# A SwiGLU kernel on one core: products three and four of each Strassen unit in 64-row tiles, and a new order around them

## The chip, the cores and the metric

The kernel runs on one core of a Trainium2 chip. The metric is the device time of one execution in microseconds (us); the median of three runs is given. Engines: PE is TensorE (matmuls; PEld is its weight load), DVE is VectorE, ACT is ScalarE, POOL is GpSimd, SP is SyncE, which issues the DMAs.

## The reference

With x of 2048 x 512 and weights of 512 x 1376 and 1376 x 512, all bf16:

```
g = silu(x @ w_gate)
u = x @ w_up
return (g * u) @ w_down
```

## The kernel before, in words

**Tiling.** The 2048 rows of x are four chunks c of 512 (SC); x stands transposed in `xT_sb`, with the 512 features as four blocks of 128 partitions (KD = 4, KH = 2). The 1376 hidden columns are ten blocks ft of 128 (NFF) and a rest of 96. First phase: for every ft and c, gate and up are products of four matmuls of 128x128 weights on 128x512 data, silu and a multiplication give h (`h0_sb` for chunks 0 and 1, `h1_sb` for 2 and 3). Second phase (`down`): h times w_down, with four 32-row matmuls side by side in the array (`strips`, line 731), a part in whole matmuls (line 780), then copies and stores.

**Classic groups.** `classic(c, fts, own)` (line 452) computes gate and up of one block directly: two column tiles of 64 side by side (line 407) or, with banks of its own, whole matmuls (line 418); then silu on ACT and the multiplication on DVE. The rest of 96 columns goes through `plan_x`, `plan_y` and `y_out` (silu pieces into `sgx_sb` and `sgy_sb`, products into `htx_sb`, `hty_sb`, `hl_sb`).

**Strassen units.** A unit (pi, u) takes two blocks ft (f0, f1 = 2u, 2u+1) and two chunks (c0, c1 = 2pi, 2pi+1), for gate (m = 0) and up (m = 1). It needs seven products instead of eight. `w_sums` builds four sums of weight blocks (S1 to S4) and a copy of A22 in `ss_sb`, mostly on POOL; `x_sums` builds T1 to T4 and a copy of B22 in `tt_sb`. These are f32 values, and their products run in a one-pass f32 format: `four` (line 585, matmuls at line 590), for each m two matmuls (k = 0, 1) of 128x128 weights on 128x512 data. Products one and two use the bf16 operands: `two` (line 597, matmuls at line 602).

A unit has three pairs of PSUM banks, one bank for each m: X (banks 0, 1 or 2, 3 by turns), Y (4, 5) and W (6, 7). `p1` writes X; ACT copies X0 into Y0 and DVE X1 into Y1. `p6` adds S2 x T2 onto X, and ACT keeps X in `r_sb`. `p2` adds onto Y, and `direct` makes an h block of it: silu of the gate bank on ACT, times the up bank on DVE. `p5` writes S1 x T1 into W. `p7` adds S3 x T3 onto X, ACT keeps X again, and `sums` makes an h block: DVE adds the kept values and W into `ts_sb`, ACT takes silu, POOL multiplies. `p4` adds A22 x T4 onto X, then `direct`; `p3` adds S4 x B22 onto W, then `sums`.

**What sets the order.** The operations are recorded in a `Plan`. Those of TensorE and of SP keep the order in which the program states them; those of ACT, DVE and POOL are put in order by `schedule`, a list planner that takes the operation that can start first by stated costs (216 ns for a bf16 matmul, 231 for an f32 one, 485 on ACT, 610 on DVE), then by priority. `emit` adds the semaphore waits. A matmul group that needs a result of an earlier group of TensorE itself (`after`) also waits on TensorE's semaphore.

**The order on TensorE**, from line 835: classic groups, among them ft 0 to 3 of chunk 1 in 64-column tiles; `plan_x` and `plan_y`; p1 of unit 0; ft 4 of chunk 1 as whole matmuls in banks 6 and 7; then for each of seven units p6, p2, p5, p7, p1 of the next unit (in the last one ft 5 of chunk 1), p4, p3; then `down`.

Of the kernel before, what the change touches and what calls it, by code (L numbers as in the profile page):

```python
# [4 lines left out]
ACT = mybir.ActivationFunctionType  # L5
# [8 lines left out]
PE_STEP, PE_STEP4, PE_LAG = 216, 231, 205  # L14
A_BUSY, A_LAG = 485, 180
# [14 lines left out]
class Plan:  # L30
# [73 lines left out]
    def emit(self, engines, sems):  # L104
        for op in self.ops:
            for d in op.deps:
                if d.dma is None and not (d.eng == op.eng == "P" and d not in op.raw):
                    d.users += 1
        for e, ops in self.order.items():
            n = 0  # L110
            for op in ops:
                if op.dma is None and op.users:
                    n += 1
                    op.count = n
        known = {e: {} for e in self.order}
        ready = {}
        done = set()
        at = dict.fromkeys(self.order, 0)
        left = len(self.ops)
        plans = {e: [] for e in self.order}  # L120
        while left:
            moved = False
            for e, ops in self.order.items():
                while at[e] < len(ops) and all(d in done for d in ops[at[e]].deps):
                    op = ops[at[e]]
                    need = {}
                    for d in op.deps:
                        if d.dma is not None:
                            key, n = d.dma
                        elif d.eng == e == "P" and d not in op.raw:  # L130
                            continue
                        else:
                            key, n = d.eng, d.count
                        if known[e].get(key, 0) < n and need.get(key, (0, 0))[0] < n:
                            need[key] = (n, d)
                    implied = {}
                    for key, (n, d) in need.items():
                        for k, v in ready[d].items():
                            if k != key:
                                implied[k] = max(implied.get(k, 0), v)  # L140
                    waits = [(d.end, key, n) for key, (n, d) in need.items() if implied.get(key, 0) < n]
                    for key, (n, d) in need.items():
                        for k, v in ready[d].items():
                            known[e][k] = max(known[e].get(k, 0), v)
                    clock = dict(known[e])
                    if op.dma is not None:
                        clock[op.dma[0]] = max(clock.get(op.dma[0], 0), op.dma[1])
                    elif op.count:
                        clock[e] = max(clock.get(e, 0), op.count)
                    ready[op] = clock  # L150
                    plans[e].append((sorted(waits, key=lambda w: w[0]), op))
                    done.add(op)
                    at[e] += 1
                    left -= 1
                    moved = True
            assert moved
        for e, steps in plans.items():
            for waits, op in steps:
                for _, key, n in waits:
                    engines[e].wait_ge(sems[key], n)  # L160
                ins = op.emit(engines[e])
                if op.dma is not None:
                    ins.then_inc(sems[op.dma[0]], 16)
                elif op.count:
                    ins.then_inc(sems[e], 1)


def bass_standalone__swiglu_ffn__prompt_kernel(nc, x, w_gate, w_up, w_down, out):
# [4 lines left out]
    KH = KD // 2  # L173
# [11 lines left out]
    HC = P // 2  # L185
# [12 lines left out]
    with ExitStack() as es:  # L198
# [21 lines left out]
        sgy_sb = [sb(f"sgy_sb{i}", [P, SC], FP32) for i in range(2)]  # L220
        o_all = sb("o_sb", [P, NOS, D], BF16)
        ss_sb = sb("ss_sb", [P, NSLOT, 5, 2, KH, P], F32R)
        tt_sb = [tt0_sb, sb("tt1_sb", [P, 5, KH, SC], F32R)]
        psum = ps("psum", [P, NB, 512], FP32)
        turn = [0, 2, 1, 3, 4, 5, 6, 7]
        bank = lambda i: psum[:, i, :]
# [77 lines left out]
        for c in range(NSC):  # L304
            load(
                f"wdx{c}",
                lambda e, c=c: e.dma_start(wdt_sb[R * c:R * (c + 1), 1, :], w_down[F - R:F, :]),
                [f"wdx{c}"], 800, 300,
            )
        for i in range(2):  # L310
            load(
                f"wdy{i}",
                lambda e, i=i: e.dma_start(wdt_sb[2 * R * i:2 * R * (i + 1), 0, :], w_down[NFF * P:F - R, :]),
# [9 lines left out]
            b = A_BUSY if engs == "A" else D_BUSY  # L323
            return plan.add(engs, emit, reads, writes, busy or b, A_LAG if engs == "A" else D_LAG, prio, after=after)

        def silu_op(out, src, reads, writes, prio=5):
            return plan.add(
                "A", lambda e: e.activation(out, src, ACT.Silu), reads, writes, A_BUSY, A_LAG, prio  # L328
            )

        def tt_op(engs, out, a, b, alu, reads, writes, prio, busy, after=()):
# [9 lines left out]
        def pe(emit, reads, writes, n, step=PE_STEP, after=()):  # L341
            return plan.add("P", emit, reads, writes, int(n * step), PE_LAG, dma=None, after=after)
# [37 lines left out]
        for dk in range(KD):  # L380
            keys = [("b", 2 * dk), ("b", 2 * dk + 1)] if dk < KD - 1 else [("b", 6)]
            pe(transposes(dk), ["xn", "ident"], keys, 0.5)
            out, src = xT_sb[:, dk, 0:HT], tview_last()
            if dk < KD - 1:
                out, src = out.rearrange("p (i h t) -> p h i t", i=NXN, h=2), tview(dk)
            else:
                out = out.rearrange("p (i t) -> p i t", i=NXN)
# [64 lines left out]
        def classic(c, fts, own=None):  # L452
            gates = [next_bank() for ft in fts] if own is None else own[:1]
            ups = [next_bank() for ft in fts] if own is None else own[1:]
            for ft, b in zip(fts, gates):
                gu_group(0, ft, c, b, own is not None)
            for ft, b in zip(fts, ups):
                gu_group(1, ft, c, b, own is not None)
            for ft, bg, bu in zip(fts, gates, ups):
                classic_out(ft, c, bg, bu)  # L460
# [3 lines left out]
        def yblk(c):  # L464
            return (0, 64) if c % 2 == 0 else (64, 128)

        def plan_x(c, b):
            def emit(e):
                for dk in range(KD):
                    for m in (0, HC):  # L470
                        ins = e.matmul(
                            psum[m:m + HC, b, :], lhsT=w_sb[:, dk, 0, XC0 + m:XC0 + m + HC],
                            rhs=xT_sb[:, dk, c * SC:(c + 1) * SC],
                            start=(dk == 0), stop=(dk == KD - 1), tile_position=(0, m),
                        )
                return ins
            pe(emit, x_keys(c) + [f"wg{slab_of[NFF]}", "wut"], [("b", b)], KD)
            y0, y1 = yblk(c)
            sgx, kx = sgx_sb[c % 2], ("sgx", c % 2)
            silu_op(sgx[96:128, :], psum[64:96, b, :], [("b", b)], [kx], 4)  # L480
            silu_op(sgy_sb[c // 2][y0:y1, :], psum[0:64, b, :], [("b", b)], [("sgy", c)], 4)
            tt_op(
                "D", htx_sb[R * c:R * (c + 1), :], sgx[96:128, :], psum[96:128, b, :], ALU.mult,
                [kx, ("b", b)], [("htx", c)], 4, D_BUSY,
            )
            if c == LC:
                tt_op(
                    "D", hl_sb[2 * R:3 * R, :], sgx[96:128, SC - P:SC], psum[96:128, b, SC - P:SC], ALU.mult,
                    [kx, ("b", b)], [("hl", 2)], 4, 300,
                )  # L490
# [27 lines left out]
        W_SUM = {"S1": 0, "S2": 1, "S3": 2, "S4": 3, "A22": 4}  # L518
        X_SUM = {"T1": 0, "T2": 1, "T3": 2, "B22": 3, "T4": 4}
# [56 lines left out]
        class Unit:  # L576
# [61 lines left out]
                    self.two(m, KH, self.Y[m], False)  # L638
                self.direct(self.Y, self.f0, self.c0)

            def p4(self):
                for m in range(2):
                    self.four("P4", m, "A22", "T4", self.X[m], False)
                self.direct(self.X, self.f1, self.c0)

            def p3(self):
                for m in range(2):
                    self.four("P3", m, "S4", "B22", self.W[m], False)
                self.sums(2, self.f0, self.c1)

            def direct(self, b, ft, c):
                sg, ksg = ring("sg", sg_sb)
# [30 lines left out]
        for at in range(NST):  # L683
            j, c = divmod(at, NSC)
# [151 lines left out]
        early = [2 * u + i for u in range(NFF // 2) if u not in U_ORDER[0] for i in range(2)]  # L836
        sums = w_sums(0, 8, (), "A")
        for fts in [[2, 3]] + [[ft] for ft in early[4:]]:
            classic(0, fts)
        for ft in early[:-2]:  # L840
            classic(1, [ft])
        sums = x_sums(0, "D", 6, sums)
        for u in U_ORDER[0]:
# [16 lines left out]
        y_out(1, 3)  # L860
        unit = make(0)
        unit.p1()
        classic(1, early[-2:-1], [6, 7])
        for n in range(len(units)):
            unit.p6()
            free = 2 * (1 - n % 2)
            unit.p2()
            unit.p5()
            unit.p7()
            if n + 1 < len(units):  # L870
                after = make(n + 1)
                after.p1()
            else:
                classic(1, early[-1:], [free, free + 1])
            unit.p4()
            unit.p3()
            unit = after
        down()

# [32 lines left out]
```

## Time and profile before

| | |
|---|---|
| runs (us) | 117.9, 118.03, 118.01; median 118.01 |
| the profiled execution's own time | 118.01 us |
| its span, first to last instruction | 116.7 us |
| granted TensorE clock | 1.000 |
| TensorE busy | 113.5 us, 97% of the span |
| DVE, ACT, POOL busy | 55.5, 55.0, 54.1 us |

The profile is one execution. A group of the page has line, engine and operation, what is written and read, the tile of the array in use (rows*columns), the shape, the count, then busy time and the mean of one in ns, then the idle time ahead of it with what ended it. Matmuls overlap in the array, so the mean of one is longer than the distance from one to the next. In the timeline the first number is the start and the second the length, in us; neighbours of one group are merged with their count. The chain of work that ended last goes from the first instruction to the last, at each step over what was waited for.

### The profile page before, as it was taken

Reading aid. Unit: us, or ns where it says so; the run is one execution under the profiler, and the core shown is the slowest. Engines: PE = TensorE matmul, PEld = TensorE weight load, DVE = VectorE, ACT = ScalarE, POOL = GpSimd, SP = SyncE. Lnnn points to the kernel's source line nnn. Section 1 sums busy time; section 2 is a strip of 40 time slices with the busy share of each in tenths; the row PEclk is TensorE's granted clock in tenths of the full one; section 3 lists DMA queues with packets and bytes.
Section 4 is the critical chain, followed back from the end, with each engine's and each line's share of the span. In section 5 each row is a group of like instructions: output and inputs, shape, how many; then the busy total and the mean of one; then the engine's idle time right before and its main releaser. Section 6 shows DMA issues by size and latency. Waiting matters only on the chain.

```text
span 116.7 us, 2563 instructions
## 1 busy us (share of the span) xinstructions
PE 113.5 (97%) x1066; PEld 65.3 (56%) x1066; DVE 55.5 (48%) x87; ACT 55.0 (47%) x104; POOL 54.1 (46%) x71
## 2 busy tenths in 40 slices
PE   7999999999899999999999999999999999999993
PEld 2695555554467666666767676554444444444452
DVE  0104599655947766685949586570000030404331
ACT  5336275389848786767676777740000020303001
POOL 1484000699994999899999942343000000000000
DMA  3999999993000000000000000000000041050512
GB/s 84 231 275 267 232 277 191 224 357 107 0 0 0 0 3 8 0 0 0 3 0 0 0 0 0 0 6 0 6 0 6 0 140 45 7 178 32 192 45 90
DMA packets 17467, 8.77 MB, mean 75 GB/s; under 512 B 8624, under 2 KB 17328, under 8 KB 17456
## 3 DMA queue, kind: packets, MB, share of 16 engines
q1 hardware_dynamic: 17312, 8.51, 28.9%
q8 instruction: 8, 0.13, 0.5%
q10 hardware_dynamic: 144, 0.10, 0.3%
q14 instruction: 3, 0.02, 0.1%
HBM read 4.68 MB, written 2.10 MB: 58 GB/s over the span
## 4 chain that ended last, share of the span: by engine, by line
PE 86%; POOL 9%; DVE 2%; ACT 1%; issue 0%
PE psum L590 28%; PE psum L731 25%; PE psum L407 12%; PE psum L602 10%; POOL ss_sb L333 9%; PE psum L780 8%; PE psum L346 2%; PE psum L418 1%; DVE tt_sb L333 1%; DVE h_sb L333 1%; ACT sg_sb L328 1%; PE psum L369 0%; PE psum L376 0%; ACT ss_sb L524 0%; DVE o_sb L322 0%
## 5 line engine op out<-in xcount | busy, mean ns | idle before, releaser
L590 PE MATMUL psum<-tt_sb,ss_sb 128*128 128x512 f32 x140 | 37.9, 414 | 0.5 <-POOL ss_sb L333 0.5
L590 PEld LDWEIGHTS psum<-tt_sb,ss_sb 128*128 128x128 f32 x140 | 26.2, 188 | 7.9 <-POOL ss_sb L333 1.1
L731 PE MATMUL psum<-wd_sb,h_sb 32*128 32x512 bf16 x480 | 27.5, 374 | 0.0
L333 DVE TENSOR_TENSOR h_sb<-sg_sb,psum 128x512 bf16<-128x512 f32 x26 | 17.8, 686 | 15.6 <-ACT sg_sb L328 10.2
L333 POOL TENSOR_TENSOR h_sb<-sg_sb,ts_sb 128x512 bf16<-128x512 f32 x14 | 18.0, 1288 | 9.6 <-ACT sg_sb L328 9.5
L333 DVE TENSOR_TENSOR ts_sb<-r_sb,psum 128x512 f32<-128x512 f32 x28 | 17.9, 681 | 7.0 <-ACT r_sb L321 7.0
L321 ACT ACTIVATE r_sb<-psum 128x512 f32<-128x512 f32 x28 | 15.3, 595 | 12.3 <-PE psum L590 12.3
L322 DVE CAST o_sb<-psum 128x512 bf16<-128x512 f32 (+1 forms) x11 | 6.4, 604 | 30.2 <-PE psum L731 25.1
L333 POOL TENSOR_TENSOR ss_sb<-w_sb 128x256 fp32r<-128x256 bf16 x20 | 13.1, 673 | 15.4 <-DVE tt_sb L333 11.6
L731 PEld LDWEIGHTS psum<-wd_sb,h_sb 32*128 32x128 bf16 x480 | 12.0, 93 | 13.8 <-PE psum L731 0.9
L328 ACT ACTIVATE sg_sb<-psum 128x512 f32<-128x512 f32 x26 | 15.6, 599 | 8.6 <-PE psum L407 8.1
L321 ACT ACTIVATE o_sb<-psum 128x512 bf16<-128x512 f32 (+1 forms) x7 | 3.7, 580 | 32.5 <-PE psum L731 25.4
L407 PE MATMUL psum<-xT_sb,w_sb 128*64 128x512 bf16 (+1 forms) x192 | 18.4, 355 | 0.0
L407 PEld LDWEIGHTS psum<-xT_sb,w_sb 128*64 128x64 bf16 x192 | 11.3, 115 | 6.8 <-DVE xT_sb L322 0.2
L602 PE MATMUL psum<-xT_sb,w_sb 128*128 128x512 bf16 x56 | 14.5, 382 | 0.0
L328 ACT ACTIVATE sg_sb<-ts_sb 128x512 f32<-128x512 f32 x14 | 8.9, 635 | 1.4 <-DVE ts_sb L333 1.4
L780 PE MATMUL psum<-wd_sb,h_sb 128*128 128x512 bf16 (+2 forms) x60 | 8.9, 308 | 0.0
L602 PEld LDWEIGHTS psum<-xT_sb,w_sb 128*128 128x128 bf16 x56 | 4.4, 98 | 7.2 <-issue 3.9
L780 PEld LDWEIGHTS psum<-wd_sb,h_sb 128*128 128x128 bf16 x60 | 4.6, 98 | 4.6 <-issue 0.4
L333 POOL TENSOR_TENSOR ss_sb<-ss_sb,w_sb 128x256 fp32r<-128x256 f32 x10 | 6.6, 674 | 0.0
L333 POOL TENSOR_TENSOR ss_sb<-w_sb,ss_sb 128x256 fp32r<-128x256 bf16 x10 | 6.5, 677 | 0.0
L322 DVE COPY psum<-psum 128x512 f32<-128x512 f32 x7 | 4.8, 693 | 0.0
(44 smaller groups left out, 62.8 us busy)
## 6 DMA issues: line engine op xcount, KB each, us to landing
out_dram<-o_sb SPq DMA_DIRECT2D x15, 128.0 KB, 1.8
wd_sb<-in_w_down_dram SPq DMA_DIRECT2D x1, 1280.0 KB, 7.7
w_sb<-in_w_gate_dram SPq DMA_DIRECT2D x4, 256.0 KB, 4.2
w_sb<-in_w_up_dram SPq DMA_DIRECT2D x4, 256.0 KB, 4.5
w_sb<-in_w_gate_dram SPq DMA_DIRECT2D x1, 352.0 KB, 5.0
w_sb<-in_w_up_dram SPq DMA_DIRECT2D x1, 320.0 KB, 4.4
xn_sb<-in_x_dram SPq DMA_DIRECT2D x1, 256.0 KB, 2.8
wdt_sb<-in_w_down_dram SPq DMA_DIRECT2D x4, 32.0 KB, 5.9
```

Source lines behind the costliest of these rows:

```text
L321: return e.activation(out, src, ACT.Copy)
L322: return e.tensor_copy(out, src)
L328: "A", lambda e: e.activation(out, src, ACT.Silu), reads, writes, A_BUSY, A_LAG, prio
L333: engs, lambda e: e.tensor_tensor(out, a, b, alu), reads, writes, busy,
L346: e.matmul(bank(NB - 1), lhsT=ones_w, rhs=ones_m, start=True, stop=True)
L407: ins = e.matmul(psum[h:h + HC, b, n0:n1], lhsT=w_sb[:, dk, m, ft * P + h:ft * P + h + HC], rhs=xT_sb[:, dk, c * SC + n0:c * SC + n1], sta ...
L418: ins = e.matmul(bank(b), lhsT=w_sb[:, dk, m, ft * P:(ft + 1) * P], rhs=xT_sb[:, dk, c * SC:(c + 1) * SC], start=(dk == 0), stop=(dk == KD ...
L590: ins = e.matmul(bank(dst), lhsT=s[:, k, :], rhs=t[:, k, :], start=(start and k == 0), stop=(k == KH - 1), skip_group_check=True,)
L602: ins = e.matmul(bank(dst), lhsT=w_sb[:, k0 + k, m, f:f + P], rhs=xT_sb[:, k0 + k, c:c + SC], start=(start and k == 0), stop=(k == KH - 1) ...
L731: ins = e.matmul(psum[:, g["bank"], 0:c1 - c0], lhsT=h(r, g["t"]), rhs=w[R * r:R * (r + 1), c0:c1], start=(start and n == 0), stop=final, ...
L780: ins = e.matmul(psum[:, b, 0:c1 - c0], lhsT=hrows(fk, t, 0, P), rhs=wd_sb[:, fk, c0:c1], start=(start and n == 0), stop=(stop and n == NF ...
```

## The change

Products three and four of a unit become one step, `p34`. Each f32 matmul of 128 rows is split into two of 64 rows: rows 0 to 63 work on one of the two outputs (gate or up), rows 64 to 127 at the same time on the other, in another bank. In a second phase the halves are exchanged, so that each output gets its missing rows. The four halves run in the order W, X, W, X; each second half waits for the first half of its own banks (`mark`). All four outputs then end within the second phase.

Around it, p2 moves behind p5 and p7. The classic group of ft 3 in chunk 1 goes from the 64-column tiles to whole matmuls ahead of p6 of the first unit, and that of ft 4 from there to behind that p6, in banks 2 and 3. The planner's cost of the silu pieces in `plan_x` rises from 485 to 610.

```diff
-        def silu_op(out, src, reads, writes, prio=5):
+        def silu_op(out, src, reads, writes, prio=5, busy=A_BUSY):
...
-            silu_op(sgx[96:128, :], psum[64:96, b, :], [("b", b)], [kx], 4)
-            silu_op(sgy_sb[c // 2][y0:y1, :], psum[0:64, b, :], [("b", b)], [("sgy", c)], 4)
+            silu_op(sgx[96:128, :], psum[64:96, b, :], [("b", b)], [kx], 4, 610)
+            silu_op(sgy_sb[c // 2][y0:y1, :], psum[0:64, b, :], [("b", b)], [("sgy", c)], 4, 610)
...
-            def p4(self):
-                for m in range(2):
-                    self.four("P4", m, "A22", "T4", self.X[m], False)
+            def half(self, a, b, dst, phase, start, after):
+
+                def emit(e):
+                    for k in range(KH):
+                        for h, m in ((0, phase), (HC, 1 - phase)):
+                            ins = e.matmul(
+                                bank(dst[m]), lhsT=ss_sb[h:h + HC, self.slot, W_SUM[a], m, k, :],
+                                rhs=tt_sb[self.pi][h:h + HC, X_SUM[b], k, :],
+                                start=(start and phase == 0 and k == 0), stop=(phase == 1 and k == KH - 1),
+                                tile_position=(h, 0), skip_group_check=True,
+                            )
+                    return ins
+                keys = [("ss", self.slot, a, m) for m in range(2)]
+                keys += [("tt", self.pi, X_SUM[b], k) for k in range(KH)]
+                return pe(emit, keys, [("b", d) for d in dst], KH, PE_STEP4, after)
+
+            def p34(self):
+                mark = [(), ()]
+                for phase in range(2):
+                    for i, (a, b, dst) in enumerate([("S4", "B22", self.W), ("A22", "T4", self.X)]):
+                        mark[i] = [self.half(a, b, dst, phase, False, mark[i])]
+                self.sums(2, self.f0, self.c1)
                 self.direct(self.X, self.f1, self.c0)
-
-            def p3(self):
-                for m in range(2):
-                    self.four("P3", m, "S4", "B22", self.W[m], False)
-                self.sums(2, self.f0, self.c1)
...
-        for ft in early[:-2]:
+        for ft in early[:-3]:
             classic(1, [ft])
...
-        classic(1, early[-2:-1], [6, 7])
+        classic(1, early[-3:-2], [6, 7])
         for n in range(len(units)):
             unit.p6()
-            free = 2 * (1 - n % 2)
-            unit.p2()
+            if n == 0:
+                classic(1, early[-2:-1], [2, 3])
             unit.p5()
             unit.p7()
+            unit.p2()
             if n + 1 < len(units):
                 after = make(n + 1)
                 after.p1()
             else:
+                free = 2 * (1 - n % 2)
                 classic(1, early[-1:], [free, free + 1])
-            unit.p4()
-            unit.p3()
+            unit.p34()
             unit = after
```

More of the change, by code (lines that the diff above doesn't have):

```diff
@@ L324, in copy_op @@
             return plan.add(engs, emit, reads, writes, busy or b, A_LAG if engs == "A" else D_LAG, prio, after=after)
-        def silu_op(out, src, reads, writes, prio=5):
+        def silu_op(out, src, reads, writes, prio=5, busy=A_BUSY):
             return plan.add(
-                "A", lambda e: e.activation(out, src, ACT.Silu), reads, writes, A_BUSY, A_LAG, prio
+                "A", lambda e: e.activation(out, src, ACT.Silu), reads, writes, busy, A_LAG, prio
             )
```

## The prediction

> **What bounds the kernel now.** I read the page first, for who is busy; then the chain of work that ended last, in order of time, for how long each kind of matmul keeps TensorE; then narrow windows of the timeline wherever that chain breaks.
>
> ```profile
> span 116.7 us, 2563 instructions
> ...
> PE 113.5 (97%) x1066; PEld 65.3 (56%) x1066; DVE 55.5 (48%) x87; ACT 55.0 (47%) x104; POOL 54.1 (46%) x71
> ...
> L590 PE MATMUL psum<-tt_sb,ss_sb 128*128 128x512 f32 x140 | 37.9, 414 | 0.5 <-POOL ss_sb L333 0.5
> ```
>
> TensorE is busy for 97% of the span, so the end moves only with TensorE's own time or with its few gaps. The f32 matmuls of line 590 are the largest group. Their mean of 414 ns runs from first column in to last result out; consecutive ones overlap, so the pace has to come from the chain:
>
> ```profile
> 53 pieces in order of time: start us, us, what
> ...
> 31.80 0.71 PE psum L590 x2
> 32.51 0.88 PE psum L602 x4
> 33.39 1.86 PE psum L590 x8
> 35.25 0.88 PE psum L602 x4
> 36.13 2.79 PE psum L590 x12
> ...
> 73.58 1.74 PE psum L418 x8
> 75.32 1.85 PE psum L590 x8
> 77.16 28.80 PE psum L731 x520
> ```
>
> From 31.80 to the stores the pieces touch: no wait is left there. The paces are 1.86 / 8 = **0.232 us** for an f32 matmul and 1.74 / 8 = **0.2175** for a bf16 one. A group of four bf16 behind f32 takes 0.88 where 4 x 0.2175 = 0.87, so a change from f32 to bf16 costs some 0.015 (0.88 is rounded). The output phase (L731) packs four 32-row matmuls side by side: the kernel issues 528 of them there (the trace holds 520), 132 steps in 28.80 = 0.218 each. Bf16 row tiles side by side thus run at the pace of one whole matmul.
>
> One gap is left, at the start of the Strassen units (PE's timeline):
>
> ```profile
> 28.91 1.89 PE L418 MATMUL psum<-xT_sb,w_sb 128*128 128x512 bf16 x8
> 30.52 0.75 PE L590 MATMUL psum<-tt_sb,ss_sb 128*128 128x512 f32 x2
> 31.80 0.71 PE L590 MATMUL psum<-tt_sb,ss_sb 128*128 128x512 f32 x2 [0.54 <-POOL ss_sb L333]
> 32.35 1.04 PE L602 MATMUL psum<-xT_sb,w_sb 128*128 128x512 bf16 x4
> ```
>
> Eight bf16 from 28.91 end their streaming at 30.65, four f32 would end at 31.58, and L602 would start near 31.60. It starts at 32.35: **0.75 us** lost. The chain blames POOL, but the sums that p6 needs (S2) were long there; what ends just before the restart is DVE's copy into the second Y bank, which must have read X before p6 adds to it:
>
> ```profile
> 22.76 1.30 POOL L333 TENSOR_TENSOR ss_sb<-ss_sb,w_sb 128x256 fp32r<-128x256 f32 x2
> ...
> 29.30 0.59 ACT L328 ACTIVATE sgy_sb<-psum 64x512 f32<-64x512 f32 x1
> ...
> 30.96 0.69 DVE L322 COPY psum<-psum 128x512 f32<-128x512 f32 x1
> ```
>
> **The change, part by part.**
>
> *Moved classic groups.* Sixteen 64-column matmuls (ft 3, chunk 1) leave the stretch ahead of the tail columns, sixteen whole ones frame p6 where eight did. Eight column-tile steps take 25.35 to 27.08 = 1.73 us in the row below, eight whole ones 1.74: no difference. But PE comes to p6 1.73 us earlier, with as much work as before between p1 and p6.
>
> ```profile
> 25.35 1.89 PE L471 MATMUL psum<-xT_sb,w_sb 128*64 128x512 bf16 x16
> 27.08 0.38 PE L497 MATMUL psum<-xT_sb,w_sb 128*64 128x512 bf16 x2
> ```
>
> ACT's sgy for the Y bank's old content ended at 29.89 (29.30 + 0.59). In the new order one cast less and the Y0 copy more stand ahead of it, about the same time, so it ends near 28.16 when all of it moves up with PE. DVE's copy now stands ahead of hty instead of behind it: 28.26 to 28.95. PE asks for it when it loads p6's second output, at 30.65 + 0.23 - 1.73 = 29.15, and the sums of POOL are there since 24.06. It is ready by 0.1 to 0.2 us, so I take the gap as gone: **-0.75**. If that cover fails, a few tenths come back. The sixteen matmuls behind p6 also give the W banks time before p5. The costs of 610 for the silu pieces only change the plan's order, which is counted here.
>
> *p2 behind p7.* PE's own work is the same. L602 comes in one group of eight (p2, p1) instead of two of four, so f32 to bf16 happens once per unit instead of twice: 7 x 0.015 = **-0.1**. What it could add is a wait: p34's first instruction adds to W after DVE has read W for the sums, and behind it on PE stands everything. In the unit that I checked:
>
> ```profile
> 46.20 1.86 PE psum L590 x8
> ...
> 47.63 1.09 ACT L321 ACTIVATE r_sb<-psum 128x512 f32<-128x512 f32 x2 [0.64 <-PE psum L590]
> ...
> 48.26 1.28 DVE L333 TENSOR_TENSOR ts_sb<-r_sb,psum 128x512 f32<-128x512 f32 x2 [0.99 <-ACT r_sb L321]
> ```
>
> p7's streaming ends at 48.05, the additions at 49.54, 1.5 us later. In the new order p2 and p1 lie between, 8 x 0.2175 = 1.74, so it is hidden by 0.2 us. p5 follows p6 directly and needs the additions of p34's W; W is now the third of four groups in p34, 0.46 us ahead of its end, so they are through some 0.95 us after p34; p6 alone covers 0.93 and the turn of shape below 0.2 more. Cost zero, by small margins (a rival below).
>
> *p3 and p4 in row tiles.* Eight whole f32 matmuls per unit become sixteen of 64 rows, eight side-by-side pairs; 7 units, 56 pairs for 56 whole ones. No row shows an f32 row tile. Bounds: the bf16 pace, 0.2175 (the 0.015 of f32 goes away), and two matmuls one after the other, 0.464. I take 0.232: the bf16 tiles of L731 run at the pace of the whole bf16 matmul, so the f32 ones should run at the pace of the whole f32 one. **0**; the ends are -0.8 and +13.0.
>
> *The exchange.* Each second half waits until the first half of its own banks is finished; the other product's two pairs lie between. L731 shows the price of such a wait with one step between:
>
> ```profile
> 85.52 0.39 PE L731 MATMUL psum<-wdt_sb,hty_sb 32*128 32x512 bf16 x4
> 85.77 0.39 PE L731 MATMUL psum<-wd_sb,h_sb 32*128 32x512 bf16 x4
> ```
>
> 0.25 instead of 0.218. With two f32 pairs between (0.46) against a matmul's 0.41 from start to finish it should cost nothing; at most 14 x 0.03 = 0.4.
>
> *Two turns of the array's shape per unit.* This is the new cost. Three places of the trace change shape:
>
> ```profile
> 27.73 0.38 PE L497 MATMUL psum<-xT_sb,w_sb 128*64 128x512 bf16 x2
> 28.04 0.39 PE L602 MATMUL psum<-xT_sb,w_sb 128*128 128x512 bf16 x1
> ...
> 76.77 0.39 PE L590 MATMUL psum<-tt_sb,ss_sb 128*128 128x512 f32 x1
> 77.09 0.40 PE L731 MATMUL psum<-wd_sb,h_sb 32*128 32x512 bf16 x4
> ...
> 105.57 0.39 PE L731 MATMUL psum<-wd_sb,h_sb 32*128 32x512 bf16 x4
> 105.89 0.39 PE L780 MATMUL psum<-wd_sb,h_sb 128*128 128x512 bf16 x1
> ```
>
> 0.31 to 0.32 from start to start, where the step alone is 0.2175 or 0.232: **0.09** each, whether rows or columns change. And the first weights of the new shape load only then. What such a load costs shows in the timeline of the loads:
>
> ```profile
> 28.04 0.11 PEld L602 LDWEIGHTS psum<-xT_sb,w_sb 128*128 128x128 bf16 x2 [0.41 <-issue]
> ...
> 31.77 0.19 PEld L590 LDWEIGHTS psum<-tt_sb,ss_sb 128*128 128x128 f32 x1 [0.94 <-POOL ss_sb L333]
> 31.77 0.30 PEld L590 LDWEIGHTS psum<-tt_sb,ss_sb 128*128 128x128 f32 x2 [0.94 <-POOL ss_sb L333]
> ```
>
> and in the page's groups, where the last number ahead of the second bar is the mean of one in ns:
>
> ```profile
> L590 PEld LDWEIGHTS psum<-tt_sb,ss_sb 128*128 128x128 f32 x140 | 26.2, 188 | 7.9 <-POOL ss_sb L333 1.1
> L602 PEld LDWEIGHTS psum<-xT_sb,w_sb 128*128 128x128 bf16 x56 | 4.4, 98 | 7.2 <-issue 3.9
> L731 PEld LDWEIGHTS psum<-wd_sb,h_sb 32*128 32x128 bf16 x480 | 12.0, 93 | 13.8 <-PE psum L731 0.9
> ```
>
> A load starts when the matmul before has started, so the distance of two loads with nothing ahead is what the first costs: 0.30 - 0.19 = **0.11** in f32, 0.11 - 0.10 = 0.01 in bf16. In the middle of a stream it hides under the matmul; behind a turn it is open. Both sides of p34 load f32 (p34 itself, then p6 of the next unit). Whether 64 rows load in half the time no row shows in f32; in bf16 32 rows take 93 ns against 98 for 128, so I keep 0.11 (half of it for p34's loads would be 0.4 less in all). The Trainium skill, "TensorE: Matmul & The Clock Gate", section LDWEIGHTS, says the same of rows: a load's time follows its columns (columns over 1.2, an estimate of 107 ns for 128), whatever the rows; by it the sum stays, and the bf16 rows agree. A turn thus costs 0.09 + 0.11 = 0.20. There are 7 into p34 and 6 out of it; the seventh goes into the output strips, which turned the array before too. 13 x 0.20 = **+2.6**.
>
> *Sum*, against the profiled execution's own time of 118.01 (span 116.7), which is also the median of the three runs: -0.75 - 0.1 + 0 + 2.6 = +1.75, **119.7 us**.
>
> **The rivals.**
>
> *Row tiles at the bf16 pace.* If the 0.015 that f32 takes per step is the weight load's and two halves hide it, 56 x 0.015 = 0.8 goes: 118.9. For it: the load is the only thing in which f32 differs in the records. Against: the pace of f32 also holds where bf16 follows and no load runs beneath.
>
> *Faster: the turn is half as dear and the pairs are quick.* If the second tile's f32 load goes under the first tile's matmul and the first is not open either, a turn costs 0.09: 13 x 0.09 = 1.2, and with pairs at 0.2175, 118.01 - 0.85 + 1.2 - 0.8 = 117.5. The point from which it decides: with such pairs the change gains as long as a turn stays under (0.85 + 0.8) / 13 = 0.13. Against it speaks the 0.11 between the loads at 31.77.
>
> *The loads don't hide in row tiles.* If a tile's next weights wait until its own rows have finished, every pair shows its load: 56 x 0.11 = +6.2 on the forecast, 125.9. Against it: L731's four tiles load every step and keep 0.218. The Trainium skill, same page, Part 3 (Packing small matmuls), states such a rule: weight loads overlap running matmuls only in other row groups; it speaks against this change, and L731's rows disagree with it.
>
> *The tiles do not run side by side in f32*, so the change is not what it says: 56 x 0.232 = +13.0, 132.7. No row speaks for or against but L731, in bf16.
>
> *Small new waits.* The covers of 0.1 to 0.2 above fail (the additions on W before p34, the exchange, the X banks in front of the second strips of the output): 0.1 to 0.25 per unit, 120.4 to 121.5. DVE and ACT are half idle, which speaks against; the margins speak for.
>
> **How the numbers follow.** Forecast, 119.2 to 120.3 with the exchange's ends: 0.50. Bf16 pace, about 118.9: 0.15. Small waits, 120.4 to 121.5: 0.13. A turn of 0.09 with today's f32 pace, 118.01 - 0.85 + 1.2 = 118.3: 0.07. Faster, 117.5: 0.07. Loads open: 0.03. Serial: 0.05. The range 118.2 to 121.6 leaves out the last three, 0.15. A measurement of this kernel tells about 0.2% from no change, 0.24 us here: faster by that are the faster rival less its upper edge, 0.06; within it (117.8 to 118.2) that edge and the lower half of the 118.3 case, 0.05; slower is the rest, 0.89.
>
> **What would show it.** Each p34 should show its first f32 load about 0.31 behind the last bf16 start, the first real pair 0.11 later, pairs 0.232 apart; p6 behind it 0.43 after the last pair. No idle PE before p6's second output. The groups of eight L602 should take 1.76. The forecast is wrong if pairs are not 0.22 to 0.24 apart, if a load of 64 rows is much shorter, or if PE waits for DVE ahead of p34.

## The result, and the profile after

The changed kernel takes 119.53 us (median of 4 runs, 118.99 to 119.71) against 118.02 before (117.9 to 118.23): ratio 1.0131, 95% interval 1.0093 to 1.0169. By the ratio that is slower by 1.5 us (1.1 to 2.0); 119.7 was forecast. Its profiled execution took 119.71, with a span of 118.3.

The page of the changed kernel, in the lines that answer to those of before (line numbers behind the diff are shifted: 745 was 731, 646 is `half`):

```profile
span 118.3 us, 2643 instructions
...
PE 115.5 (98%) x1114; PEld 63.9 (54%) x1114; DVE 55.6 (47%) x87; ACT 55.4 (47%) x104; POOL 54.1 (46%) x71
...
L590 PE MATMUL psum<-tt_sb,ss_sb 128*128 128x512 f32 x84 | 21.7, 405 | 0.0
...
L646 PE MATMUL psum<-tt_sb,ss_sb 64*128 64x512 f32 x112 | 14.8, 404 | 0.0
...
L646 PEld LDWEIGHTS psum<-tt_sb,ss_sb 64*128 64x128 f32 x112 | 10.0, 184 | 4.8 <-DVE ts_sb L333 2.1
```

The 56 f32 matmuls of products three and four have become 112. One of 64 rows takes as long as one of 128 did (404 ns here; 414 before), and its weight load too (184 against 188). The chain of work that ended last, from the start of the units on:

```profile
27.27 1.73 PE psum L418 x8
29.00 0.93 PE psum L590 x4
29.93 1.74 PE psum L418 x8
31.67 1.85 PE psum L590 x8
33.52 1.74 PE psum L602 x8
35.26 2.07 PE psum L646 x16
37.33 3.00 PE psum L590 x12
40.33 1.74 PE psum L602 x8
42.07 2.07 PE psum L646 x15
44.14 2.96 PE psum L590 x12
```

The gap ahead of p6's second output is gone: four f32 take 0.93 without a break. Eight bf16 in a row take 1.74. But sixteen tiles take 2.04 to 2.07 where eight whole f32 matmuls took 1.86, and the twelve f32 behind them 2.96 to 3.00 instead of 2.76 to 2.79. That is one turn of the array's shape in each. The timeline of PE around one p34 shows the first part of that turn, the wait of the new shape:

```profile
41.69 0.38 PE L602 MATMUL psum<-xT_sb,w_sb 128*128 128x512 bf16 x1
42.00 0.50 PE L646 MATMUL psum<-tt_sb,ss_sb 64*128 64x512 f32 x2
...
42.34 0.40 PE L646 MATMUL psum<-tt_sb,ss_sb 64*128 64x512 f32 x2
...
42.00 2.14 PE L646 MATMUL psum<-tt_sb,ss_sb 64*128 64x512 f32 x16
44.07 0.50 PE L590 MATMUL psum<-tt_sb,ss_sb 128*128 128x512 f32 x1
```

The timeline of the loads, in two windows, shows the second part, the load that nothing hides:

```profile
42.00 0.19 PEld L646 LDWEIGHTS psum<-tt_sb,ss_sb 64*128 64x128 f32 x2 [0.42 <-DVE ts_sb L333]
...
42.00 0.30 PEld L646 LDWEIGHTS psum<-tt_sb,ss_sb 64*128 64x128 f32 x4 [0.42 <-DVE ts_sb L333]
```

From the last bf16 start (41.69) to the first load of the new shape pass 0.31. The second pair's loads begin 0.30 - 0.19 = 0.11 behind the first's, and the second pair starts at 42.34, 0.34 behind the first: 0.11 more than a step. The remaining steps are even: the sixteen end at 44.14, and the last pair's start lies 0.39 to 0.40 ahead of that at some 43.74, so six steps take 1.40, **0.234 each**. DVE's name behind the load is only the latest semaphore. DVE's additions end at 41.82 (40.53 + 1.29), before the load, and the load starts 0.31 behind the last matmul's start, as in the turns of before (0.31 to 0.32).

### The profile page after: what moved, and what is told of

The parts are those of the page before. It is cut to its first block, busy times and chain, and to the rows that moved or that the text cites. A ratio compares the mean times of both kernels' runs of the same rounds, so it can differ in the third digit from the quotient of the medians.

```text
span 118.3 us, 2643 instructions
## 1 busy us (share of the span) xinstructions
PE 115.5 (98%) x1114; PEld 63.9 (54%) x1114; DVE 55.6 (47%) x87; ACT 55.4 (47%) x104; POOL 54.1 (46%) x71
## 4 chain that ended last, share of the span: by engine, by line
PE 94%; DMA 3%; SPq 1%; issue 0%; DVE 0%
PE psum L745 24%; PE psum L590 17%; PE psum L407 13%; PE psum L646 12%; PE psum L602 10%; PE psum L794 7%; PE psum L418 4%; DMA w_sb<-in_w_up_dram 3%; PE psum L471 3%; PE psum L497 1%; SPq L265 0%; SPq L282 0%; DVE o_sb L322 0%; PE psum L800 0%
## 5 line engine op out<-in xcount | busy, mean ns | idle before, releaser
L590 PE MATMUL psum<-tt_sb,ss_sb 128*128 128x512 f32 x84 | 21.7, 405 | 0.0
L590 PEld LDWEIGHTS psum<-tt_sb,ss_sb 128*128 128x128 f32 x84 | 15.3, 188 | 5.5 <-issue 2.2
L407 PE MATMUL psum<-xT_sb,w_sb 128*64 128x512 bf16 (+1 forms) x176 | 16.3, 342 | 0.1
L646 PE MATMUL psum<-tt_sb,ss_sb 64*128 64x512 f32 x112 | 14.8, 404 | 0.0
L602 PE MATMUL psum<-xT_sb,w_sb 128*128 128x512 bf16 x56 | 13.5, 381 | 0.0
L407 PEld LDWEIGHTS psum<-xT_sb,w_sb 128*64 128x64 bf16 x176 | 9.6, 110 | 6.5 <-DMA w_sb<-in_w_up_dram 0.3
L646 PEld LDWEIGHTS psum<-tt_sb,ss_sb 64*128 64x128 f32 x112 | 10.0, 184 | 4.8 <-DVE ts_sb L333 2.1
L602 PEld LDWEIGHTS psum<-xT_sb,w_sb 128*128 128x128 bf16 x56 | 4.8, 98 | 7.0 <-issue 2.3
```

The lines of the kernel that those rows point to most:

```text
L407: ins = e.matmul(psum[h:h + HC, b, n0:n1], lhsT=w_sb[:, dk, m, ft * P + h:ft * P + h + HC], rhs=xT_sb[:, dk, c * SC + n0:c * SC + n1], sta ...
L590: ins = e.matmul(bank(dst), lhsT=s[:, k, :], rhs=t[:, k, :], start=(start and k == 0), stop=(k == KH - 1), skip_group_check=True,)
L602: ins = e.matmul(bank(dst), lhsT=w_sb[:, k0 + k, m, f:f + P], rhs=xT_sb[:, k0 + k, c:c + SC], start=(start and k == 0), stop=(k == KH - 1) ...
L646: ins = e.matmul(bank(dst[m]), lhsT=ss_sb[h:h + HC, self.slot, W_SUM[a], m, k, :], rhs=tt_sb[self.pi][h:h + HC, X_SUM[b], k, :], start=(st ...
```

## The experiments

The theory is the prediction's: the order saves 0.85, 13 turns of 0.20 cost 2.6, the tiles themselves nothing. The rivals: the loss is per pair or in the exchange; or the order saves nothing and the tiles cost only what was lost. Ratios are to the kernel before on the same chip; "above before" is the ratio less one, times 118.0.

**The order without the tiles.** In the changed kernel, with `p4` and `p3` in whole matmuls as they were (the planner's cost of 610 stays in):

```diff
-            unit.p34()
+            unit.p4()
+            unit.p3()
```

> The new order alone: p3 and p4 stay whole matmuls, p4 then p3. Turns theory (the order gains 0.75 from the gap ahead of p6's second output and 0.1 from fewer f32 to bf16 changes; the row tiles lose 2.6 by 13 turns of the array's shape): 0.85 below the kernel before, about 117.2 where that is 118.0. Rival (the order gains nothing here, and the tiles lose only the 1.5 that the changed kernel lost): no change, 118.0.

Measured: 118.35 us, ratio 1.0039 (1.0016 to 1.0061), 0.5 above before. The theory missed by 1.3. Its chain shows where the gain went, 20 f32 matmuls in a row that should take 20 x 0.232 = 4.64:

```profile
35.22 4.80 PE psum L590 x20
40.02 1.74 PE psum L602 x8
41.77 4.86 PE psum L590 x20
```

Six such groups take 4.80, 4.86, 4.79, 4.85, 4.86 and 4.86, together 1.2 too much. The loads and DVE in the second of them:

```profile
44.37 0.30 PEld L590 LDWEIGHTS psum<-tt_sb,ss_sb 128*128 128x128 f32 x2 [0.26 <-DVE ts_sb L333]
44.97 0.53 PEld L590 LDWEIGHTS psum<-tt_sb,ss_sb 128*128 128x128 f32 x3 [0.30 <-DVE ts_sb L333]
```

```profile
43.03 0.69 DVE L333 TENSOR_TENSOR h_sb<-sg_sb,psum 128x512 bf16<-128x512 f32 x1
43.64 1.28 DVE L333 TENSOR_TENSOR ts_sb<-r_sb,psum 128x512 f32<-128x512 f32 x2
```

p5 overwrites W, and now stands straight behind p6. W, written last by p3, is still to be read by DVE's two additions, and these stand behind the product of X (43.03), which was ready first. So the new wait is p5's on W. In the old order p2 covered it. PE's matmuls around it start at 44.15, 44.37, 44.71, 44.97 and 45.31. The distances up to the two loads, 0.23 and 0.26, are hardly more than a step of 0.23; the ones behind them, 0.33 and 0.34, hold an f32 load of 0.10 each. So nearly all of the 0.2 that this unit loses is the two loads that could start only when DVE was through, and little of it the waiting itself.

**The same with W first.**

```diff
-            unit.p4()
             unit.p3()
+            unit.p4()
```

> The new order with whole matmuls, but p3 (W) ahead of p4 (X), so that W is through 0.93 before the unit's end. The run with p4 ahead of p3 lost some 0.2 per unit where p5, now straight behind p6, waits for DVE's additions on W, and the 0.11 of an f32 load behind each such wait. If that is what ate the gain of the order, it is back here: 0.85 below the kernel before, about 117.1 to 117.2. Rival (the order's gain at the gap was never there, or is lost to the later landing of x): as that run, 118.3, or 118.0.

Measured: 116.72, ratio **0.9928** (0.9904 to 0.9953), 0.85 below before, as the theory had it. The same part of its chain:

```profile
41.55 4.61 PE psum L590 x20
46.16 1.74 PE psum L602 x8
47.91 4.56 PE psum L590 x20
```

So the order, with the planner's cost of 610 in it, is worth its 0.85 if W is finished ahead of X; how much of that is the cost alone comes below. Against this kernel, which has the changed kernel's order of W and X but whole matmuls, the tiles cost (1.0131 - 0.9928) x 118.0 = 2.4 us; 2.6 were forecast. With the two intervals that is 2.4 give or take 0.5; in the profiled executions the stretch from p1 to the output strips is 2.8 longer (52.46 against 49.65).

**The tiles in the old order.** In the kernel before, with the pairs in the order X, W:

```diff
-            unit.p4()
-            unit.p3()
+            unit.p34()
```

> The row tiles alone, in the old order of the steps, halves in the order X, W, X, W so that W's additions have time. Turns theory: 13 turns of 0.20 on 118.0, 120.6, and up to 0.1 per unit more where PE waits for DVE's additions on W, since only p1 lies between p7 and the tiles: 120.6 to 121.3; the gap of 0.75 ahead of p6's second output is still there. Rival (tiles lose only 1.5): 119.5.

Measured: 122.14, ratio 1.0357 (1.033 to 1.0384), 4.2 above before: slower than either theory said. The waits of PE's loads (us in total, times, the longest) name the rest:

```profile
PEld psum L646 <- DVE ts_sb L333: 2.2, 5, 0.4
PEld psum L646 <- ACT r_sb L321: 2.1, 5, 0.4
```

The five for DVE's additions lie in the middle of p34, each some 0.17 beyond the step, and behind each the next pair's step is 0.10 longer, because the f32 load started only when the wait ended. The first unit's p34 has such a wait too, so six of the seven units have it: 2.6 + 6 x 0.27 = 4.2. The five for ACT's copies are turns into the tiles, with ACT's semaphore as the latest. I had set up to 0.1 for a wait on DVE, without the load behind it.

**Two turns more per unit.**

```diff
             unit.p2()
+            unit.p34(0)
             if n + 1 < len(units):
...
-            unit.p34()
+            unit.p34(1)
```

(first halves X, W; second halves W, X.)

> The changed kernel with the same 56 pairs, but the first halves (X, W) ahead of p1 and the second halves (W, X) behind it, so each unit turns the array twice more: once into whole bf16 matmuls (0.09 + 0.01) and once back into f32 tiles (0.09 + 0.11). Turns theory: 7 x 0.30 = 2.1 above the changed kernel, about 121.6. Rival (the loss is in the tiles or in the exchange, per pair): as the changed kernel, 119.5, or a little less since the exchange is further away.

Measured: 124.05, ratio 1.0498 (1.0469 to 1.0528), 4.3 above the changed kernel; 2.1 were forecast. The loads of one unit:

```profile
41.45 0.30 PEld L646 LDWEIGHTS psum<-tt_sb,ss_sb 64*128 64x128 f32 x4 [0.42 <-ACT r_sb L321]
42.19 0.30 PEld L646 LDWEIGHTS psum<-tt_sb,ss_sb 64*128 64x128 f32 x4 [0.43 <-DVE ts_sb L333]
42.85 0.55 PEld L602 LDWEIGHTS psum<-xT_sb,w_sb 128*128 128x128 bf16 x4 [0.37 <-issue]
43.82 0.76 PEld L646 LDWEIGHTS psum<-tt_sb,ss_sb 64*128 64x128 f32 x8 [0.42 <-PE psum L602]
44.95 0.19 PEld L590 LDWEIGHTS psum<-tt_sb,ss_sb 128*128 128x128 f32 x1 [0.36 <-POOL tt_sb L333]
```

Each of the four turns (41.45, 42.85, 43.82, 44.95) is there, so 0.30 more per unit holds. Beyond it stands the load at 42.19, which waits for DVE's additions on W, 0.16 and its own open 0.10, 7 x 0.26 = 1.8, and 0.1 more in the first unit. 2.1 + 1.9 = 4.0; the stretch from p1 to the output strips is 4.1 longer than in the changed kernel (56.56 against 52.46). PE also waited some 0.4 for x's last chunk near the start, but it came to p1 no later than in the changed kernel (25.99 against 26.30), so that is no part of the loss. The per-pair rival, which said no change, falls, but as a measure of the turn alone this run is spoiled.

**The turn on a bf16 load.** p2 and the next p1 in row tiles too, in six of seven units, by a function like `half` on `w_sb` and `xT_sb`, in the order Y, X, Y, X:

```diff
-            unit.p2()
             if n + 1 < len(units):
                 after = make(n + 1)
-                after.p1()
+                unit.p21(after)
```

> The changed kernel with p2 and the next unit's p1 in bf16 row tiles as well (Y, X, Y, X, exchanged), in six of the seven units. The turn into the tiles then comes on a bf16 load and the first f32 load of p34 hides under bf16 tiles. Turns theory with the open f32 load: 6 x (0.11 - 0.01) = 0.6 below the changed kernel, about 118.9. Rival A (a turn costs 0.20 whatever is loaded): as the changed kernel, 119.5. Rival B (the loss grows with the number of tile pairs): 48 pairs more, 1.3 to 2 above it, 121.

Measured: 118.76, ratio 1.0069 (1.0041 to 1.0098), 0.7 below the changed kernel by the ratios, with 48 pairs more; their intervals overlap by a hair, so the trace carries it. Its chain:

```profile
46.48 1.83 PE psum L646 x16
48.31 1.84 PE psum L670 x16
50.15 2.97 PE psum L590 x12
```

Eight bf16 pairs with the turn take 1.83, 0.09 over eight whole ones (1.74). The f32 tiles behind them take 1.84 (1.91 and 1.86 in the first two units) instead of 2.04 to 2.07: no turn, no open load. The way back (2.97) is as dear as before. A pair of tiles costs nothing by itself; the open f32 load is half of the turn.

**The exchange without its cover.** In `p34` of the changed kernel the two loops change places, so the halves run W, W, X, X:

```diff
-                for phase in range(2):
-                    for i, (a, b, dst) in enumerate([("S4", "B22", self.W), ("A22", "T4", self.X)]):
+                for i, (a, b, dst) in enumerate([("S4", "B22", self.W), ("A22", "T4", self.X)]):
+                    for phase in range(2):
```

> The changed kernel with the halves in the order W, W, X, X, so that nothing lies between a first half and its exchange. If the exchange's wait is real and only hidden by the other product: the load starts 0.40 + 0.07 behind the last pair's start and costs 0.11 more, 0.58 instead of 0.23, so 14 x 0.35 = 4.9 above the changed kernel, 124.4. Rival (the wait costs the 0.03 that the output strips show): 14 x 0.03, 119.9.

Measured: 124.23, ratio 1.0556 (1.052 to 1.0593), 5.0 above the changed kernel. Two loads of each unit now wait for an earlier matmul of TensorE:

```profile
43.10 0.77 PEld L646 LDWEIGHTS psum<-tt_sb,ss_sb 64*128 64x128 f32 x8 [0.50 <-PE psum L646]
44.37 0.30 PEld L646 LDWEIGHTS psum<-tt_sb,ss_sb 64*128 64x128 f32 x4 [0.50 <-PE psum L646]
```

The wait is real (14 of them, two per unit: 5.0 / 14 = 0.35 each) and the other product hides it.

**What closed the gap?** Two edits on the kernel before, one with the planner's cost alone, one with the moved classic groups alone (cost 485, p2 in its old place):

```diff
-            silu_op(sgx[96:128, :], psum[64:96, b, :], [("b", b)], [kx], 4)
+            silu_op(sgx[96:128, :], psum[64:96, b, :], [("b", b)], [kx], 4, 610)
```

(and likewise for `sgy`)

> The kernel before with one edit: the silu pieces of the tail columns cost 610 instead of 485 in the planner. ACT's copy then stands ahead of the last silu piece and DVE's copy ahead of hty. Plan theory (the gap ahead of p6's second output is DVE's copy standing behind hty): the copy comes about 0.6 to 0.7 earlier, gap gone, 0.7 below the kernel before, 117.3. Rival (the gap goes because a classic group leaves the stretch ahead of it): no change, 118.0.

```diff
-        for ft in early[:-2]:
+        for ft in early[:-3]:
...
-        classic(1, early[-2:-1], [6, 7])
+        classic(1, early[-3:-2], [6, 7])
...
             unit.p6()
+            if n == 0:
+                classic(1, early[-2:-1], [2, 3])
```

> The kernel before with the two classic groups moved alone; p2 stays behind p6, the planner's cost stays 485, p3 and p4 whole. Plan theory: PE and the ACT chain both come 1.73 earlier, DVE's copy still stands behind hty, so the gap of some 0.75 stays: 118.0. Rival: gap gone, 117.3.

Measured: the cost alone 116.59, ratio **0.9921** (0.9888 to 0.9953); the groups alone 117.72, ratio 1.0006 (0.998 to 1.0032). With the cost alone, DVE's copy stands ahead of hty, and the chain has p6's four matmuls without a break:

```profile
29.48 0.70 DVE L322 COPY psum<-psum 128x512 f32<-128x512 f32 x1 [0.30 <-ACT sgy_sb L328]
30.20 0.69 DVE L333 TENSOR_TENSOR hty_sb<-sgy_sb,psum 128x512 bf16<-128x512 f32 x1
...
30.18 0.92 PE psum L590 x4
```

With the groups alone it stands behind hty, and PE's second output of p6 waits for it:

```profile
28.41 0.69 DVE L333 TENSOR_TENSOR hty_sb<-sgy_sb,psum 128x512 bf16<-128x512 f32 x1
29.02 0.69 DVE L322 COPY psum<-psum 128x512 f32<-128x512 f32 x1
...
29.86 0.71 PE L590 MATMUL psum<-tt_sb,ss_sb 128*128 128x512 f32 x2 [0.52 <-DVE psum L322]
```

The copy ends at 29.71 and PE starts p6's second output at 29.86, behind the same gap; everything came earlier together. The gap is a matter of the planner's order alone. The kernel with W first has the cost of 610 too, and it is no faster (0.9928) than the cost alone makes the kernel before (0.9921). So the medians show no gain of the moved groups and the moved p2 themselves.

## Why the prediction was right, point by point

- **The gap, -0.75.** Right in size: gone in the changed kernel, and -0.9 (-0.6 to -1.3 by the interval) where the cost that closes it is the only edit. The prediction gave the moved groups, fewer casts and the copy's place together as reason; the groups have no part in it (1.0006). That PE asks at 29.15 and the copy is ready before held, with less room than the 28.95 of the prediction: the copy ran to 28.99 in the changed kernel.
- **p2 behind p7, -0.1.** Eight L602 take 1.74. No run's time separates so little. In the trace of the kernel with W first a unit takes 4.56 + 1.74 = 6.30 from the third on, against 6.38 to 6.41 in the kernel before, so some 0.1 per unit where 0.015 was forecast: late in those 20 f32 matmuls the steps are 0.227, not 0.232. Why is open; the changed kernel has no f32 group of that length. The wait ahead of p34, taken as hidden by 0.2, was so: DVE's additions end at 41.82 and the load that needs them starts at 42.00. That p5 then stands without cover was seen, and "Cost zero, by small margins" held: the changed kernel has no wait at p5. The size of what that saves was not seen: whole matmuls with X first lose 1.2 there. The tiles, and the turns behind them, give part of their price back against that order, which is why it lies only 1.1 below the changed kernel.
- **Pairs, 0.** 0.234 against 0.232: 56 x 0.002 = 0.1. The rivals with the bf16 pace, open loads and serial tiles fall. The rule in the Trainium skill, "TensorE: Matmul & The Clock Gate", Part 3 (What overlaps and what doesn't), that loads overlap only matmuls of other row groups, disagrees with these rows too.
- **The exchange, 0.** Right; 5.0 without the other product between.
- **The turns, 13 x 0.20.** Shown in the trace by their parts (0.31 from start to load, 0.11 for the load), and by the kernel whose tiles turn on bf16. An f32 load of 64 rows is as dear as one of 128 (184 and 188 ns), as the prediction took it. The Trainium skill, same page, section LDWEIGHTS, says so too: the rows don't matter to a load's time. The two kernels that differ only in the tiles are 2.4 apart by their times and 2.8 in their traces (2.6 was forecast).
- **Not in the sum:** PE comes to the tail columns 1.73 earlier, and so closer to the landing of x's last chunk. In the profiled execution its load waited there,

```profile
24.39 0.57 PEld L471 LDWEIGHTS psum<-xT_sb,w_sb 128*64 128x64 bf16 x8 [0.44 <-DMA xT_sb<-in_x_dram]
```

some 0.12 beyond the step. That chunk landed at 22.62 in the profiled execution of before, at 24.34 in that of the changed kernel, at 21.38 in that of the tiles on bf16. Whether this makes the changed kernel's runs spread (0.7) is not shown: the 24 runs of before beside the last experiments spread by 1.05 (117.11 to 118.16).

The sum of +1.75 (119.76 us, written down as 119.7) against the measured +1.5 (1.1 to 2.0) is right by its own steps; the one that it had partly wrong is what closes the gap, not how much that is worth.

## What to carry to other kernels

A change of the array's shape is a cost of its own, and dearest in front of a slow weight load: keep one shape through a stretch, or turn on an operand whose load is short. Before an order is praised or a layout blamed, look at which copy or addition reads the bank that is overwritten next; finishing that bank first was worth 1.3 us, nearly as much as the whole change lost. Where a list planner sets the order, a stated cost that is 20% low can place one operation wrongly: correcting it alone gave the fastest kernel here, 0.9921, which needs neither tiles nor a new order and beats both kernels, as does the new order with W first (0.9928; the two intervals are alike).

## What the runs showed of the hardware that was not expected

A wait ahead of an f32 weight load costs more than the wait: the load, 0.10 to 0.11, is then open as well. In the tiles of the old order that made 0.17 into 0.27, in six of seven units. In the order without the tiles, with X first, two waits that were over within 0.03 of their step cost 0.24 in this way in the unit shown.
